# Attention weights transposed on TensorE instead of by DMA, and the division by the row sum moved behind the product with v

## The chip, the cores and the metric

The kernel runs on one core of one Trainium2 chip. The metric is device time in microseconds (us), the median of several executions. Engines are named as in the profile: PE (TensorE, matrix products and transposes, written to PSUM), PEld (its weight loads), DVE (VectorE), ACT (ScalarE), POOL (GpSimd, which here works only on SBUF) and SP (SyncE, which issues the DMAs).

## The reference

Attention with a causal window of 128 and a linear bias by head, then two gated feed-forward blocks over the 2304 tokens.

```python
# q, k, v: (4, 8, 576, 64); window = 128
scores = scale * np.matmul(q, k.transpose(0, 1, 3, 2))
mask = (rel >= 0) & (rel < window)
scores = np.where(mask, scores + bias[None], -1000000000.0)
scores = scores - np.max(scores, axis=-1, keepdims=True)
attn = np.exp(scores)
attn = attn / (np.sum(attn, axis=-1, keepdims=True) + 1e-09)
x = np.matmul(attn, v)            # then to (2304, 512)
x = (x @ w_a * (x @ w_b)) @ w_out                 # d_ff 1536
out = (x @ w1 * (x @ w2)) @ w3 @ moe2_w_out       # d_ff 1024
```

## The kernel before

**Attention.** A unit is one batch and one pair of heads, so there are 16. A unit has 576 queries: four blocks of 128 and a last one of 64. Blocks are taken in runs, (0, 1), (2, 3) and (4,), three to a unit, 48 in all. For a block of queries only one or two blocks of 128 keys lie in the window. The two heads are `j`; for the last block both heads share the 128 partitions.

- `prep` (L268 to L273) transposes the raw q and k of the next unit on PE and splits them into a high and a low part.
- `scores` (L311) makes three products per block and head. `step_exps` (L337, L343) adds the bias, finds the row maximum on DVE, and takes exponentials on ACT with their row sums in `st`. The tile `pe` holds the exponentials in float32, queries on partitions.
- `norms` (L356, L359) makes the reciprocal of the row sums, times 2^15 (`PSC`).
- `probs` (L371 to L382) multiplies the exponentials by it and splits them into two float16 parts in the tile `pp`: the high part on ACT (L375; block 0 on DVE, L371), the low part on DVE (L377). One DMA transpose per block (L382, on SP's queue) turns `pp` into `pt`, with keys on partitions.
- `pv` (L408) multiplies with v, which is in three bfloat16 parts, in five products per head and key block. `pv_out` (L422, L423) scales by 2^-15 and splits the result into `x_hi` (ACT) and `x_lo` (DVE).

**What sets the order.** `attention_ops` makes steps, one per run. Step n holds the late operations of the step before, then scores and exponentials of run n, `probs` of run n-1, the transposes of `prep`, a slot for filler work (None), and `pv` of run n-`LAG`. In the slot, up to 2.4 us (`FILL`) of products of the first feed-forward group (L545, L571) are put in, for tokens whose attention is done. Conversions of the weights are spread over the steps. During the first three units `keep_warm` (L352) adds products that nothing uses. A scheduler then orders each engine's instructions by its own estimates of time. The PSUM pool `ps_t` has three buffers, used in turn by the tiles of `prep` and of `pv`.

**After attention** what is left of the first group follows, then the other nine groups in tiles of 512 tokens (L545, L582, L597), and the product of w3 with the last weight (L453, L461), all on PE with the splits on ACT, DVE and POOL.

Of the kernel before, what the change touches and what calls it, by code (L numbers as in the profile page):

```python
# [8 lines left out]
F32 = mybir.dt.float32  # L9
# [25 lines left out]
LAG = 3  # L35
# [7 lines left out]
def attention_moe_moe(ctx, tc, q, k, v, w_a, w_b, w_o, w_1, w_2, w_3, w_o2, out):  # L43
    nc = tc.nc
# [23 lines left out]
    def f32(ap):  # L68
        return ap.bitcast(F32)
# [284 lines left out]
    def norms(run):  # L354
        st = live.pop(run)
        nc.vector.tensor_scalar(  # L356
            out=st[:, 2], in0=st[:, 1], scalar1=1.0e-9, scalar2=1.0 / PSC, op0=ALU.add, op1=ALU.mult
        )
        nc.vector.reciprocal(out=st[:, 3], in_=st[:, 2])  # L359

    def probs(u, i):
        m, n, nb, nj = window(i)
        d = live[u, i]
        pe, st = d["pe"], d["st"][:, 3]
        pp = sm_p.tile([P, 2 * 2 * 2 * P], F16, name="pp", bufs=5)[:, 0:2 * nj * n].rearrange(
            "p (a b c) -> p a b c", a=nj, b=2
        )
# [24 lines left out]
    def pv(run):  # L392
# [258 lines left out]
    def attention_ops():  # L651

        late = []
        for n in range(NR + LAG):
# [5 lines left out]
            if 1 <= n <= NR:  # L660
                ops.append(lambda r=runs[n - 1]: norms(r))
# [17 lines left out]
            if n >= LAG:  # L679
                ops.append(lambda r=runs[n - LAG]: pv(r))  # L680
# [51 lines left out]
    warm = sm_p.tile([P, 8 * P], F16, name="pt", bufs=6)[:, 0:2 * P]  # L732
# [64 lines left out]
```

## Time and profile before

| what | value |
|---|---|
| median of three runs | 1004.87 us (1002.13 to 1005.45) |
| the profiled execution, first to last instruction | 1003.0 us |
| PE busy over the span | 961.5 us (96%) |
| DVE, ACT, POOL busy | 532.3, 430.6, 400.7 us |
| PE busy, 0 to 80 us | 65.5 us, granted clock 0.68 |
| PE busy, 80 to 250 us (rest of attention) | 149.3 us, granted clock 0.94 |
| PE busy, 330 to 1003 us | 668.8 us of 673, granted clock 1.00 |

The profiled execution has no time of its own beside its span; the span of 1003.0 us lies within the three runs, 1.9 us under their median. Attention takes the first 250 us. A clock of 1.00 is 2.4 GHz, 0.50 is 1.2 GHz. The record of a product has a modelled end which runs into the next, so that a short stall between products doesn't show as idle time. Idle time of an engine counts where the chain of work that ended last runs through it.

### The profile page before, as it was taken

How to read it: one execution, taken by the hardware profiler on the slowest of the kernel's cores; microseconds unless marked ns; L12 is line 12 of the kernel's file. 1: busy time of each engine (PE TensorE's matmuls, PEld its weight loads, DVE VectorE, ACT ScalarE, POOL GpSimd, SP SyncE). 2: the span in 40 equal slices, each digit the busy share in tenths (PEclk: the TensorE clock that was granted, in tenths of full speed). 3: DMA queues.
4: the chain of work that ended last, by engine and by line, in shares of the span. 5: the costliest groups of instructions: out<-in, count | busy, mean ns of one | idle time of the engine just before them, and what ended most of it. 6: DMA issues, size and time to landing. Idle time of an engine off the chain costs nothing.

```text
span 1003.0 us, 16251 instructions
## 1 busy us (share of the span) xinstructions
PE 961.5 (96%) x6162; PEld 803.7 (80%) x6162; DVE 532.3 (53%) x1188; ACT 430.6 (43%) x1003; POOL 400.7 (40%) x329
## 2 busy tenths in 40 slices
PE   7889898888999999999999999999999999999998
PEld 6558787777988788888888888888888888888886
DVE  5979777764689634556474462442442442422222
ACT  5768767765654434434443341343421321311110
POOL 4344212211687423545462362574741631511111
PEclk6769998988999999999999999999999999999999
DMA  5897786864433222323331240120120220000012
GB/s 128 165 185 154 145 137 138 148 119 69 147 106 115 85 85 95 95 74 105 103 118 63 73 128 22 42 84 1 42 85 1 61 66 1 22 1 1 29 64 97
DMA packets 160078, 85.21 MB, mean 85 GB/s; under 512 B 128000, under 2 KB 148992, under 8 KB 160000
## 3 DMA queue, kind: packets, MB, share of 16 engines
q1 hardware_dynamic: 160000, 84.18, 34.0%
q8 instruction: 48, 0.79, 0.3%
q14 instruction: 30, 0.25, 0.1%
HBM read 58.20 MB, written 8.91 MB: 67 GB/s over the span
## 4 chain that ended last, share of the span: by engine, by line
PE 81%; DMA 6%; DVE 6%; issue 3%; ACT 3%; POOL 1%; SPq 1%; DVEq 0%; POOLq 0%; ACTq 0%
PE mm L545 44%; PE mm L582 11%; PE mm L597 10%; PE mm L461 4%; DMA pt<-pp 4%; PE s L311 3%; PE tr L408 3%; PE tr L268 2%; PE mm L571 1%; DVE pp L377 1%; DVE ca L121 1%; DMA raw<-in_moe_w_a 1%; DVE ca L114 1%; DVE ca L117 1%; POOL ca L126 1%
## 5 line engine op out<-in xcount | busy, mean ns | idle before, releaser
L72 POOL TENSOR_TENSOR gl<-g,gh 128x512 fp32r<-128x512 f32 (+1 forms) x108 | 124.5, 1153 | 316.2 <-ACT gh L555 301.8
L552 DVE TENSOR_TENSOR g<-a,mm 128x512 f32<-128x512 f32 (+1 forms) x108 | 64.1, 594 | 214.9 <-PE mm L545 193.6
L126 POOL TENSOR_TENSOR ca<-ca,ce 128x512 int32<-128x512 int32 x76 | 101.2, 1332 | 141.6 <-ACT ce L110 65.9
L555 ACT ACTIVATE gh<-g 128x512 fp32r<-128x512 f32 (+1 forms) x108 | 60.2, 558 | 176.4 <-DVE g L552 176.2
L545 PE MATMUL mm<-x_hi,wlA 128*128 128x512 f32 (+1 forms) x464 | 107.9, 351 | 0.0
L550 ACT ACTIVATE a<-mm 128x512 f32<-128x512 f32 (+1 forms) x108 | 55.9, 519 | 121.0 <-PE mm L545 120.9
L545 PE MATMUL mm<-x_lo,whA 128*128 128x512 f32 (+1 forms) x464 | 104.2, 345 | 0.0
L545 PE MATMUL mm<-x_hi,whA 128*128 128x512 f32 (+1 forms) x464 | 103.0, 343 | 0.0
L545 PE MATMUL mm<-x_hi,wlB 128*128 128x512 f32 (+1 forms) x400 | 99.3, 370 | 2.1 <-DVE g L552 0.8
L545 PE MATMUL mm<-x_lo,whB 128*128 128x512 f32 (+1 forms) x400 | 98.6, 368 | 0.0
L545 PE MATMUL mm<-x_hi,whB 128*128 128x512 f32 (+1 forms) x400 | 98.1, 368 | 0.0
L114 DVE TENSOR_SCALAR ca<-ca 128x512 f32<-128x512 f32 x76 | 47.3, 622 | 91.6 <-ACT ca L107 89.4
L545 PEld LDWEIGHTS mm<-x_hi,wlA 128*128 128x128 f32 x464 | 77.9, 192 | 11.1 <-issue 0.4
L545 PEld LDWEIGHTS mm<-x_lo,whA 128*128 128x128 f32 x464 | 78.1, 192 | 10.6
L545 PEld LDWEIGHTS mm<-x_hi,whA 128*128 128x128 f32 x464 | 77.3, 191 | 10.3
L545 PEld LDWEIGHTS mm<-x_hi,wlB 128*128 128x128 f32 x400 | 70.8, 188 | 16.0 <-DVE g L552 1.2
L586 DVE TENSOR_TENSOR acc<-acc,mm 128x512 f32<-128x512 f32 (+1 forms) x100 | 62.0, 630 | 39.4 <-PE mm L582 39.1
L107 ACT ACTIVATE ca<-raw 128x512 f32<-128x512 f32 x76 | 50.6, 666 | 72.5 <-DMA raw<-in_moe_w 39.5
L121 DVE SCALAR_TENSOR_TENSOR ca<-raw,ca 128x512 int32<-128x512 int32 x76 | 80.6, 1060 | 1.8
L545 PEld LDWEIGHTS mm<-x_lo,whB 128*128 128x128 f32 x400 | 71.1, 188 | 12.8
L545 PEld LDWEIGHTS mm<-x_hi,whB 128*128 128x128 f32 x400 | 71.0, 189 | 12.6
L110 ACT ACTIVATE ce<-raw 128x512 int32<-128x512 uint32 x76 | 50.8, 669 | 60.0 <-POOL ca L126 25.0
(104 smaller groups left out, 1873.4 us busy)
## 6 DMA issues: line engine op xcount, KB each, us to landing
raw<-in_moe_w SPq DMA_DIRECT2D x32, 512.0 KB, 3.7
raw<-in_moe_w_out SPq DMA_DIRECT2D x20, 512.0 KB, 3.5
raw<-in_moe_w_a SPq DMA_DIRECT2D x12, 512.0 KB, 3.6
raw<-in_moe_w_b SPq DMA_DIRECT2D x12, 512.0 KB, 3.7
out<-acc SPq DMA_DIRECT2D x18, 256.0 KB, 2.0
q_raw<-in_q SPq DMA_DIRECT2D x32, 128.0 KB, 2.8
k_raw<-in_k SPq DMA_DIRECT2D x32, 128.0 KB, 2.7
v_raw<-in_v SPq DMA_DIRECT2D x32, 128.0 KB, 2.7
```

What stands on the lines that cost most here:

```text
L72: eng.tensor_tensor(out=out, in0=a, in1=b, op=ALU.subtract)
L110: nc.scalar.activation(e, lw, ACTF.Copy, scale=2.0 ** -29)
L114: nc.vector.tensor_scalar(out=a, in0=a, scalar1=bits(0x38000000), scalar2=None, op0=ALU.max)
L121: nc.vector.scalar_tensor_tensor(out=ai, in0=hw, scalar=-(1 << 30), in1=ai, op0=ALU.bitwise_and, op1=ALU.bitwise_or)
L126: nc.gpsimd.tensor_tensor(out=ai, in0=ai, in1=es[0], op=ALU.add)
L545: nc.tensor.matmul(p, w[:, z, kk, :], x[:, kk, o], start=(y == 0), stop=(y == len(terms) - 1))
L550: nc.scalar.activation(a, ps[0], ACTF.Copy)
L552: nc.vector.tensor_tensor(out=gg, in0=a, in1=ps[1], op=ALU.mult)
L555: nc.scalar.activation(gh, gg, ACTF.Copy)
L582: nc.tensor.matmul(p, w, x, start=(y == 0), stop=(y == len(terms) - 1))
L586: nc.vector.tensor_tensor(out=ya, in0=ya, in1=p, op=ALU.add)
L597: nc.tensor.matmul(p, x, w, start=(y == 0), stop=(y == len(terms) - 1))
```

## The change

`probs` no longer multiplies by the reciprocal and no longer goes through a DMA. PE transposes the float32 exponentials into a PSUM tile of `ps_t`, in pieces of 128 by 128. ACT reads that tile, scales by 2^15 and writes the high float16 part. DVE reads it again and writes the low part. `norms` moves to just ahead of `pv` of the same run; POOL then copies the reciprocals out along 64 columns for each head (`rb`). `pv` starts each block with a PE transpose of `rb` into the right half of its own PSUM tile. `pv_out` copies that half to SBUF (`rt`, DVE), multiplies the product by it (`y`, DVE), and splits `y` into `x_hi` (ACT) and `x_lo` (now POOL, helper `sub`). `LAG` is 2 instead of 3.

```diff
-LAG = 3
+LAG = 2
...
     def norms(run):
         st = live.pop(run)
         nc.vector.tensor_scalar(
-            out=st[:, 2], in0=st[:, 1], scalar1=1.0e-9, scalar2=1.0 / PSC, op0=ALU.add, op1=ALU.mult
+            out=st[:, 2], in0=st[:, 1], scalar1=1.0e-9, scalar2=PSC, op0=ALU.add, op1=ALU.mult
         )
         nc.vector.reciprocal(out=st[:, 3], in_=st[:, 2])
+        k = st.shape[2]
+        rb = sm_p.tile([P, 2 * P], F32, name="rb")[:, 0:max(k, 2) * D]
+        nc.gpsimd.tensor_copy(
+            out=rb.rearrange("p (k d) -> p k d", k=k),
+            in_=st[:, 3].unsqueeze(2).to_broadcast([P, k, max(2 // k, 1) * D]),
+        )
...
     def probs(u, i):
...
-                nc.scalar.activation(pp[:, j, 0, :], pe[:, j, :n], ACTF.Copy, scale=st[:, j:j + 1])
-        for j in range(nj):
-            nc.vector.scalar_tensor_tensor(
-                out=pp[:, j, 1, :], in0=pe[:, j, :n], scalar=st[:, j:j + 1], in1=pp[:, j, 0, :],
-                op0=ALU.mult, op1=ALU.subtract,
-            )
-        t = sm_p.tile([P, 8 * P], F16, name="pt", bufs=6)[:, 0:2 * nj * n]
-        nc.sync.dma_start_transpose(
-            out=t.rearrange("p (g m) -> p g m", m=P), in_=pp.rearrange("p a b c -> p (a b c)")
-        )
...
+        ps = ps_t.tile([P, W], F32, name="tr")[:, 0:nj * n]
+            for g in range(nb):
+                o = (j * nb + g) * P
+                nc.tensor.transpose(ps[:, o:o + P], pe[:, j, g * P:(g + 1) * P], ident)
+        t = d["pt"] = sm_p.tile([P, 2, W], F16, name="pt", bufs=6)
+        hi, lo = t[:, 0, 0:nj * n], t[:, 1, 0:nj * n]
+        nc.scalar.activation(hi, ps, ACTF.Copy, scale=PSC)
+        nc.vector.scalar_tensor_tensor(out=lo, in0=ps, scalar=PSC, in1=hi, op0=ALU.mult, op1=ALU.subtract)
...
+            nc.tensor.transpose(ps[:, 2 * P + at:3 * P + at], d["rb"], ident)
...
-        nc.scalar.activation(x_hi[:, hp, o], ps, ACTF.Copy, scale=1.0 / PSC)
-        nc.vector.scalar_tensor_tensor(
-            out=x_lo[:, hp, o], in0=ps, scalar=1.0 / PSC, in1=f32(x_hi[:, hp, o]),
-            op0=ALU.mult, op1=ALU.subtract,
-        )
+        if m > LAST:
+            nc.vector.tensor_copy(out=r, in_=ps[:, 2 * P:2 * P + m])
...
+        nc.vector.tensor_tensor(out=y, in0=ps[:, :m], in1=r, op=ALU.mult)
+        nc.scalar.activation(x_hi[:, hp, o], y, ACTF.Copy)
+        sub(nc.gpsimd, x_lo[:, hp, o], y, f32(x_hi[:, hp, o]))
...
-                ops.append(lambda r=runs[n - 1]: norms(r))
...
+                ops.append(lambda r=runs[n - LAG]: norms(r))
                 ops.append(lambda r=runs[n - LAG]: pv(r))
```

Lines of the changed kernel: L377 are the transposes of `pe`, L380 and L381 the split, L396 the transpose of `rb`, L405 the products with v, L421 or L425 the copy, L427 the product, L428 `x_hi`. L548 and L574 are the filler products that were L545 and L571.

How the order moves. On PE, in the middle of attention, a stretch from one product with v to the next scores. Before, between the last product with v and the next filler (`tr<-ident,k_raw` is `prep`'s transpose, `s` a tile of scores):

```order
L408 MATMUL tr<-pt,v_raw_96 64x128
L268 MATMUL tr<-ident,k_raw_112 128x128 x3
L311 MATMUL s<-qkl,qkh 128x128 x2
L311 MATMUL s<-qkh 128x128 x2
L311 MATMUL s<-qkh,qkl 128x256 x2
L311 MATMUL s<-qkl,qkh 128x256 x2
L311 MATMUL s<-qkh 128x256 x2
L545 MATMUL mm<-x_hi,wlA_324 128x256
```

The same part of a step now:

```order
L405 MATMUL tr<-pt,v_raw_97 64x64
L377 MATMUL tr<-ident,pe 128x128 x4
L574 MATMUL mm<-gh,wlA_368 128x256
L311 MATMUL s<-qkh,qkl 128x128 x2
L377 MATMUL tr<-ident,pe 128x128 x4
L574 MATMUL mm<-gh,wlA_776 128x256
L574 MATMUL mm<-gl,whA_367 128x256
L268 MATMUL tr<-ident,k_raw_112 128x128 x3
L311 MATMUL s<-qkl,qkh 128x128 x2
L311 MATMUL s<-qkh 128x128 x2
```

Two groups of four transposes of `pe` stand among the scores and the fillers. Over the whole of attention the 256 transposes stand in 65 groups: 24 of four, 23 of two, 16 of six or eight.

On PE, inside one `pv`, between the products of its two blocks. Before:

```order
L408 LDWEIGHTS v_raw_96
L408 MATMUL tr<-pt,v_raw_96 64x128
L408 LDWEIGHTS v_1976
L408 MATMUL tr<-pt,v_1976 64x128
L408 LDWEIGHTS v_1976
```

Now, with the transpose of `rb`:

```order
L405 LDWEIGHTS v_raw_95
L405 MATMUL tr<-pt,v_raw_95 64x128
L396 MATMUL tr<-ident,rb 128x128
L405 LDWEIGHTS v_1826
L405 MATMUL tr<-pt,v_1826 64x128
```

A float32 transpose of the whole array now stands between two rows of products that use half of its columns. There are 80 of these; each is alone.

On DVE, one step in the middle of attention. Before (`pp` is the low part, `x_lo` the result of an earlier run):

```order
L377 SCALAR_TENSOR_TENSOR pp<-pe,st,pp 128x256
L377 SCALAR_TENSOR_TENSOR pp<-pe,st,pp 128x128 x2
L377 SCALAR_TENSOR_TENSOR pp<-pe,st,pp 128x256
L273 TENSOR_TENSOR qkl<-tr,qkh 128x512
L356 TENSOR_SCALAR st<-st 128x4
L359 RECIPROCAL st<-st 128x4
L356 TENSOR_SCALAR st<-st 128x1
L359 RECIPROCAL st<-st 128x1
L423 SCALAR_TENSOR_TENSOR x_lo<-tr,x_hi 128x256 x2
```

The same kind of step now:

```order
L421 COPY rt<-tr 128x256
L427 TENSOR_TENSOR y<-tr,rt 128x256
L381 SCALAR_TENSOR_TENSOR pt<-tr,pt 128x256
L381 SCALAR_TENSOR_TENSOR pt<-tr,pt 128x512
L555 TENSOR_TENSOR g<-a,mm 128x256
L425 COPY rt<-tr 64x64
L273 TENSOR_TENSOR qkl<-tr,qkh 128x512
L425 COPY rt<-tr 64x64
L427 TENSOR_TENSOR y<-tr,rt 128x64
L381 SCALAR_TENSOR_TENSOR pt<-tr,pt 128x512
```

DVE now reads PSUM tiles of `ps_t` in three kinds of instruction (the low part L381, the copy and the product of `pv_out`, and `prep`'s L273), where `prep` and `x_lo` did before.

## Rows read from the trace of the kernel before

**Rows 1.** The page: engine totals, and the granted clock in 40 slices of 25.1 us.

```profile
PE 961.5 (96%) x6162; PEld 803.7 (80%) x6162; DVE 532.3 (53%) x1188; ACT 430.6 (43%) x1003; POOL 400.7 (40%) x329
...
PEclk6769998988999999999999999999999999999999
```

**Rows 2.** Busy time by stretch: stretch, length, engines, granted clock, DMA share, GB/s.

```profile
0.00:80.00 80.00, 65.52 (x582) 47.46 (x584) 61.42 (x225) 55.58 (x168) 31.95 (x35) 0.68 0.83 159
80.00:250.00 170.00, 149.25 (x1944) 130.83 (x1939) 124.46 (x470) 121.44 (x385) 42.58 (x39) 0.94 0.72 130
250.00:330.00 80.00, 77.93 (x472) 68.16 (x470) 61.92 (x74) 43.51 (x82) 59.29 (x45) 1.00 0.40 126
330.00:1003.00 673.00, 668.83 (x3172) 557.21 (x3172) 284.50 (x421) 210.09 (x369) 266.92 (x211) 1.00 0.19 60
...
70.00:80.00 10.00, 10.00 (x97) 8.39 (x98) 6.52 (x32) 8.61 (x29) 1.37 (x2) 0.50 1.00 171
```

**Rows 3.** Chain that ended last, shares by line: 0 to 80 us, then 80 to 250.

```profile
by line: PE s L311 18.3%; PE tr L408 10.7%; PE tr L268 9.2%; DVE pp L377 8.3%; DMA pt<-pp 7.4%; DMA raw<-in_moe_w_a 5.7%; issue 4.9%; PE mm L352 4.3%; DMA k_raw<-in_k 3.4%; DVE qkl L273 2.8%; DVE ca L114 2.7%; DVE pe L337 2.7%; DVE ca L121 
...
by line: PE mm L545 21.7%; DMA pt<-pp 18.2%; PE tr L408 12.5%; PE s L311 10.4%; PE mm L571 8.7%; PE tr L268 6.3%; DVE pp L377 4.2%; issue 3.9%; DMA k_raw<-in_k 2.2%; DMA q_raw<-in_q 2.0%; ACT pe L343 1.7%; DVE pe L337 1.7%; ACT pp L375 1.4%
```

**Rows 4.** Pieces of that chain: start, us, engine, tile, line, count; first under half clock.

```profile
10.81 1.26 PE tr L268 x5
...
126.43 4.02 DMA pt<-pp
...
132.79 0.68 PE tr L408 x20
133.47 0.48 PE tr L268 x3
...
145.58 0.59 PE tr L268 x4
146.17 1.44 PE mm L571 x12
147.60 1.24 PE tr L408 x40
...
149.39 0.33 PE tr L268 x3
```

**Rows 5.** Waits in the whole span: who for whom, total us, times, longest.

```profile
PE tr L408 <- DMA pt<-pp: 18.4, 19, 1.8
PEld L408 <- issue: 17.7, 26, 2.6
...
PEld L408 <- DMA pt<-pp: 7.7, 8, 1.6
```

**Rows 6.** Instructions by line and shape: count, busy us, mean ns, idle before.

```profile
L377 DVE SCALAR_TENSOR_TENSOR pp<-pe,st,pp 128x256 f16<-128x256 f32 x112 | 58.6, 561 | 7.6 <-ACT pp L375 7.5
L375 ACT ACTIVATE pp<-pe,st 128x256 f16<-128x256 f32 x112 | 49.4, 499 | 8.9 <-DMA pt<-pp 4.7 <-DVE ca L121 1.1 <-ACT pe L343 0.9
L72 POOL TENSOR_TENSOR gl<-g,gh 128x256 fp32r<-128x256 f32 x36 | 28.9, 803 | 90.5 <-ACT gh L555 76.1 <-DMA k_raw<-in_k 14.4
L423 DVE SCALAR_TENSOR_TENSOR x_lo<-tr,x_hi 128x256 fp32r<-128x256 f32 x32 | 13.2, 414 | 4.0 <-ACT x_hi L422 3.8
L273 DVE TENSOR_TENSOR qkl<-tr,qkh 128x512 fp32r<-128x512 f32 x16 | 10.9, 680 | 1.6 <-ACT qkh L272 1.5
L272 ACT ACTIVATE qkh<-tr 128x512 fp32r<-128x512 f32 x16 | 9.4, 590 | 7.1 <-PE tr L268 7.0
```

**Rows 7.** DMA issues by line: count, median us to landing.

```profile
pt<-pp SPq DMA_TRANSPOSE x80, 3.3
```

More of the change, by code (lines that the diff above doesn't have):

```diff
@@ L356, in norms @@
         nc.vector.tensor_scalar(
-            out=st[:, 2], in0=st[:, 1], scalar1=1.0e-9, scalar2=1.0 / PSC, op0=ALU.add, op1=ALU.mult
+            out=st[:, 2], in0=st[:, 1], scalar1=1.0e-9, scalar2=PSC, op0=ALU.add, op1=ALU.mult
         )
         nc.vector.reciprocal(out=st[:, 3], in_=st[:, 2])
+        k = st.shape[2]
[4 more added lines that the diff above has]
+        )
+        for x, s in enumerate(run):
+            live[s]["rb"] = rb[:, x * P:(x + 1) * P]
     def probs(u, i):
@@ L363, in probs @@
         d = live[u, i]
-        pe, st = d["pe"], d["st"][:, 3]
-        pp = sm_p.tile([P, 2 * 2 * 2 * P], F16, name="pp", bufs=5)[:, 0:2 * nj * n].rearrange(
-            "p (a b c) -> p a b c", a=nj, b=2
-        )
+        pe = d.pop("pe")
+        ps = ps_t.tile([P, W], F32, name="tr")[:, 0:nj * n]
         for j in range(nj):
-            if i == 0:
-                nc.vector.tensor_scalar(
-                    out=pp[:, j, 0, :], in0=pe[:, j, :n], scalar1=st[:, j:j + 1], scalar2=None, op0=ALU.mult
-                )
-            else:
-                nc.scalar.activation(pp[:, j, 0, :], pe[:, j, :n], ACTF.Copy, scale=st[:, j:j + 1])
-        for j in range(nj):
-            nc.vector.scalar_tensor_tensor(
-                out=pp[:, j, 1, :], in0=pe[:, j, :n], scalar=st[:, j:j + 1], in1=pp[:, j, 0, :],
-                op0=ALU.mult, op1=ALU.subtract,
-            )
-        t = sm_p.tile([P, 8 * P], F16, name="pt", bufs=6)[:, 0:2 * nj * n]
-        nc.sync.dma_start_transpose(
-            out=t.rearrange("p (g m) -> p g m", m=P), in_=pp.rearrange("p a b c -> p (a b c)")
-        )
-        order = "p (a b c m) -> p a b c m" if nj == 2 else "p (b c a m) -> p a b c m"
-        d["pt"] = t, t.rearrange(order, a=2, b=2, c=nb)
+            for g in range(nb):
[5 more added lines that the diff above has]
+        nc.vector.scalar_tensor_tensor(out=lo, in0=ps, scalar=PSC, in1=hi, op0=ALU.mult, op1=ALU.subtract)
     ready = [0]
@@ L413, in pv @@
             if u < WARM_UNITS and m == P:
-                keep_warm(WARM, t[:, 0:4 * P])
+                keep_warm(WARM, t[:, 0, 0:nj * nb * P])
     def pv_out(run):
@@ L420, in pv_out @@
         o = slice(b * S + i * P, b * S + i * P + m)
-        ps = outs.pop(run)[:, :m]
-        nc.scalar.activation(x_hi[:, hp, o], ps, ACTF.Copy, scale=1.0 / PSC)
-        nc.vector.scalar_tensor_tensor(
-            out=x_lo[:, hp, o], in0=ps, scalar=1.0 / PSC, in1=f32(x_hi[:, hp, o]),
-            op0=ALU.mult, op1=ALU.subtract,
-        )
+        ps = outs.pop(run)
+        r = sm_p.tile([P, 2 * P], F32, name="rt")[:, :m]
+        if m > LAST:
+            nc.vector.tensor_copy(out=r, in_=ps[:, 2 * P:2 * P + m])
+        else:
+            for j in range(2):
+                c = slice(j * D, (j + 1) * D)
+                nc.vector.tensor_copy(out=r[c], in_=ps[c, 2 * P + j * LAST:2 * P + (j + 1) * LAST])
+        y = sm_p.tile([P, 2 * P], F32, name="y")[:, :m]
+        nc.vector.tensor_tensor(out=y, in0=ps[:, :m], in1=r, op=ALU.mult)
+        nc.scalar.activation(x_hi[:, hp, o], y, ACTF.Copy)
+        sub(nc.gpsimd, x_lo[:, hp, o], y, f32(x_hi[:, hp, o]))
         if hp == NP - 1:
@@ L731, in attention_moe_moe @@
     fl = Filler()
-    warm = sm_p.tile([P, 8 * P], F16, name="pt", bufs=6)[:, 0:2 * P]
+    warm = sm_p.tile([P, 2, W], F16, name="pt", bufs=6)[:, 0, 0:2 * P]
     nc.vector.memset(warm, 0.0)
```

6 lines of the change are left out of this document (4 added, 2 removed).

## The prediction

> **What bounds the kernel now.** I read the engine totals and the clock in slices first [rows 1]: PE is busy 96% of the span, and its granted clock is above 0.9 from the slice at 251 us on, but 0.6 to 0.8 in six of the ten slices before. The busy time by stretch [rows 2] parts the span in two. From 330 us PE is busy 668.8 of 673 us at clock 1.00; nothing there is touched by the change, and nothing that happens on other engines shortens it. The change lives in attention, the first 250 us. There PE is busy 65.5 of 80 us and 149.3 of 170 us, so it has 14.5 + 20.8 = 35 us of recorded idle time in all; its clock is 0.68 and 0.94. DVE has 61.4 + 124.5 = 186 us of work, ACT 177, POOL 75. What attention is late by at its end is paid at the end of the kernel, because PE has work without gaps afterwards. The converse holds too.
>
> Who ends last in attention is told by the chain [rows 3]. From 80 us on, the five listed PE lines make 59.6% of it, and the DMA transposes (pt<-pp) 18.2% of 170 = 30.9 us. Before 80 us the chain is a mixture: PE 42.5% in its three attention lines and L352, DVE's low part 8.3%, the DMA transposes 7.4% of 80 = 5.9 us. So PE is first in both stretches, and the DMA transposes are the largest single thing beside it: 37 us together. Their latency is 3.3 us [rows 7], and single ones stand in the chain with 4.02 us [rows 4].
>
> **The change part by part.** All of it is priced in the profiled execution, span 1003.0 us; the median of the runs is 1.9 us longer.
>
> *Added on PE: transposes of the exponentials.* A unit has 2 for block 0, 4 for each of blocks 1 to 3, and 2 for block 4: 16, in 16 units 256. They are of the same kind as `prep`'s (128x128 float32 against `ident`). Mean durations of such instructions contain the pipeline, so I price them by pieces of the chain that join without a gap [rows 4]: three cost 0.48 us between a product with v and scores (0.16 each), four 0.59 (0.15 each), three before filler products 0.33 (0.11 each). 256 of them are 28 to 41 us. By the order they stand in 65 groups of about four, some before scores, some before fillers; I take 0.13, or 33 us.
>
> *Added on PE: the transposes of `rb`*, five to a unit, 80 in all, each alone. One more transpose in a group costs 0.59 - 0.48 = 0.11 us, the first of a group 0.48 - 2 x 0.11 = 0.26. Twenty products with v take 0.62 to 0.68, so a lone transpose is worth eight of them. 33 of the 80 break a row of products with v and pay 0.26 (8.6 us); 47 stand where PE changes from another kind of work anyway, and I give them 0.11 (5.2 us). That is 14 us, with bounds 9 and 21.
>
> Here a rule speaks against the change. The Trainium skill, "TensorE: Matmul & The Clock Gate", Part 4: PE-mode transpose, gives about 275 ns for a 128x128 transpose in a kernel's context. At that price the 336 would be an estimated 92 us in place of 47. The groups in the chain show 0.11 to 0.26, so the trace does not agree for transposes in groups, and only nearly for single ones.
>
> *The clock.* In the first 80 us five to six of the 16 units run at a granted clock of 0.68 [rows 2], and five transposes cost 1.26 us under half clock [rows 4], 0.25 each. 5/16 of 47 is 14.7 us, which at 0.68 is 21.6: 7 us more. The bounds are 0 (full clock) and 15 (half clock all the time).
>
> *Removed: the DMA transposes.* The chain says 37 us. PE's own waits [rows 5] say less: 18.4 on PE and 7.7 on PEld are 26, and of another 17.7 ("issue", before the products with v) nobody is named. I take 30. The 80 transposes also leave SP's queue, and loads of q and k stop waiting behind them: 2.2% + 2.0% of 170 is 7 us of the chain from 80 us on [rows 3]; I take 5, bounds 0 and 7.
>
> *DVE and ACT.* For a block of 256 keys, two low parts at 0.561 become one of 512 read from PSUM, nearest to L273's 0.680; two high parts at 0.499 become one, nearest to L272's 0.590 [rows 6]. Over 48 such blocks DVE loses 21 us and ACT 20. Per pair of blocks `pv_out` puts two DVE instructions of about 0.41 in the place of one at 0.414, so 32 x 0.41 = 13 us comes back to DVE, and some 5 us for the last blocks. DVE nets about -10 to -18 of 186, ACT about -15 of 177. In the chain the two lines are worth 6.6 + 7.1 + 2.4 = 16 us [rows 3], but new ones stand in the same places: I take -3, bounds 0 and -10.
>
> *POOL* gains 32 subtractions at 0.803 [rows 6], 16 small ones and 48 copies, at most 0.8 each: about 26 + 6 + 38 = 70 us on 75, in 250. It stays the least loaded. But `pv` now waits for `rb`, behind which conversions and v's parts (POOL is in order) may be queued; that goes into the next term.
>
> *New waits.* The pool `ps_t` keeps three buffers, but where `prep` and `pv` took two tiles a step, `probs` now takes one or two more. A transpose can wait for the split of a tile three places earlier, and `pv` for POOL's copy. No row shows this; its bounds are 0, since fillers stand between in most steps, and 25, the DMA's own waits over again. I take 5, since DVE and ACT have become lighter and the splits take 1.3 us against the 3 to 4 us of a DMA.
>
> *`LAG` 2.* One step fewer at the end, 250/51 = 4.9 us, of which PE's work stays: -4, bounds 0 and -5. By the order 34 filler products (302 instead of 336) fall behind the end of attention, 34 x 0.12 = 4 us; PE does them either way, so this is zero for the sum.
>
> Sum: 33 + 14 + 7 - 30 - 5 - 3 + 5 - 4 = +17 us, span 1020, and with the 1.9 us about **1022 us**. A check from the other side: 54 us of added PE time do not fit into 35 us of recorded idle time, of which the start and the waits for exponentials remain. So PE has to end later unless its clock rises.
>
> **The rivals.**
>
> *PE stays at full clock (faster).* In the first 80 us a clock of 0.68 costs PE 0.32 x 80 = 26 us, and from 80 to 250 us 0.06 x 170 = 10 us [rows 2]. Between 70 and 80 us PE was busy all 10 us at clock 0.50, and the slices from 75 to 150 us show a clock of 0.9 or more [rows 1]. If the denser stream of the changed kernel is granted 1.0 in most of what was half clock, the 7 us above go and some 15 to 20 of the 36 come back: 1022 - 7 - 18 = 997. It decides from a mean clock of about 0.9 in the first 80 us. Against it: [rows 1] shows 0.6 to 0.7 in the first three slices although `keep_warm` puts in products there, and 0.8 again in three of the four slices from 150 to 250 us.
>
> *The PSUM buffers take the DMA's place (slower still).* If the tiles of `ps_t` wait for ACT and DVE as long as `pt` waited for its DMA, the term of 5 is 25: 1022 + 20 = 1042, and more if PE's clock falls with the gaps.
>
> *Neutral.* If all 35 us of idle time and the DMA's waits are one and the same and fill up exactly, PE's additions are covered: 1003 to 1008.
>
> *Transposes at 0.275 us each.* Priced as mechanism of this kernel by the highest lone price under half clock, 0.25 to 0.26, for all 336: 87 us instead of 47, 1022 + 40 = 1062. The page named above would have it so; the groups at 0.11 to 0.16 speak against it.
>
> **How the numbers follow.** Forecast 0.55 (1006 to 1036); full clock 0.22 (985 to 1002); PSUM buffers 0.16 (1036 to 1060); neutral 0.05; dear transposes 0.02. About 0.3%, 3 us, is what a measurement of this kernel can tell from no change: below 1002 is faster, above 1008 slower. Faster takes the clock's 0.22; same the neutral case and a little of the forecast's edge, 0.08; slower the rest, 0.70. The range leaves out half of the clock case below 994 and the upper part of the PSUM and dear cases above 1046.
>
> **What would show it.** In the profile after: PE busy from 0 to 250 us with less idle time than 35 us, and attention's last product with v some 15 us later; L377 and L396 together near 47 us of the PE's stream; no DMA in the chain of attention but loads; granted clock of the first 80 us near 0.7. The forecast is wrong on the fast side if that clock is above 0.9, or if groups of four transposes cost no more than 0.4 us; on the slow side if L377 or L396 wait for ACT, DVE or POOL for more than some 10 us in all. From 330 us before, or its counterpart after, nothing should differ.

## The result

The changed kernel takes **1017.88 us** (median of four runs, 1016.24 to 1019.03); the kernel before took 1005.16 us beside it (four runs, 1002.13 to 1005.82). The ratio is 1.0134, with a 95% interval of 1.0112 to 1.0156: 12.7 us slower. The execution that was profiled took 1017.48 us, with a span of 1015.7 us.

The page of the changed kernel, engine totals and granted clock in 40 slices of 25.4 us, to be read beside [rows 1]:

```profile
PE 990.5 (98%) x6498; PEld 823.8 (81%) x6498; DVE 531.6 (52%) x1156; ACT 422.7 (42%) x971; POOL 443.9 (44%) x425
...
PEclk9889999999999999999999999999999999999999
```

The first slices, which read 6, 7, 6, now read 9, 8, 8, and from the fourth on there is nothing under 9. The same by stretch, with the columns of [rows 2] (length, busy PE, PEld, DVE, ACT, POOL, granted clock, DMA share, GB/s):

```profile
0.00:80.00 80.00, 65.31 (x659) 48.22 (x660) 58.40 (x203) 52.29 (x154) 47.87 (x62) 0.91 0.50 122
80.00:250.00 170.00, 167.69 (x2079) 142.11 (x2077) 117.81 (x440) 111.23 (x352) 67.32 (x101) 1.00 0.23 51
250.00:330.00 80.00, 75.65 (x526) 65.16 (x525) 63.09 (x86) 45.35 (x93) 55.27 (x46) 1.00 0.37 112
330.00:1003.00 673.00, 672.90 (x3204) 561.48 (x3203) 287.46 (x422) 213.79 (x375) 272.88 (x217) 1.00 0.18 58
```

From 80 to 250 us PE is busy 167.69 of 170 us at clock 1.00, where [rows 2] has 149.25 at 0.94. In the first 80 us it is busy as long as before (65.31 against 65.52), but at 0.91 in place of 0.68. The DMA share has fallen from 0.83 to 0.50 and from 0.72 to 0.23. The chain that ended last, 0 to 80 us and then 80 to 250 us, against [rows 3]:

```profile
by line: PE s L311 14.4%; PE tr L377 9.7%; ACT pe L343 7.7%; PE tr L268 7.4%; DMA raw<-in_moe_w_a 6.6%; PE mm L352 6.5%; PE tr L405 6.1%; issue 4.4%; DVE ca L121 3.8%; DVE ca L114 3.5%; DMA k_raw<-in_k 3.2%; DVE pt L381 3.0%; ACT ca L107 3.
...
by line: PE mm L548 20.5%; PE tr L405 17.3%; PE s L311 16.3%; PE tr L377 11.5%; PE mm L574 9.9%; PE tr L268 7.3%; PE tr L396 6.0%; ACT pe L343 2.9%; DVE pe L337 1.3%; issue 1.2%; DVE qkl L273 1.0%; DVE st L356 0.9%; ACT pt L380 0.7%; DVE y 
```

In the second stretch the listed PE lines alone are 88.8%, and no DMA stands there any more. L377 is the transposition of the exponentials, L396 that of `rb`. In the first stretch ACT's exponentials (7.7%), loads and DVE's conversions stand between the pieces of PE, as they did before.

The last product of the exponentials with v, from the timeline of each kernel (start, us, engine, line), of before and then of after:

```profile
251.14 0.20 PE L408 MATMUL tr<-pt,v_raw 128*64 128x64 f16 x2
...
257.93 0.20 PE L405 MATMUL tr<-pt,v_raw 128*64 128x64 f16 x1
```

Attention ends 6.8 us later. Behind it, the first block of products of w3 with the last weight (L461 before, L464 after, twelve in a row in the chain) starts at 345.52 us before and at 358.06 us after:

```profile
345.52 2.78 PE mm L461 x12
...
358.06 2.77 PE mm L464 x12
```

That is 12.5 us. Behind this place both kernels are alike: 1003.0 - 345.5 = 657.5 us and 1015.7 - 358.1 = 657.6 us. So all of the loss arises before it: 6.8 us up to the end of attention, and 5.7 us from there to this place. In that second stretch the first products of the feed-forward groups, from which the fillers are taken (L545 before, L548 after), are these (stretch, length, PE busy and count, clock, DMA share, GB/s):

```profile
251.30:345.50 94.20, 63.52 (x336) 1.00 0.38 118
...
258.10:358.00 99.90, 67.52 (x370) 1.00 0.37 111
```

The 34 more are the filler products that the order no longer puts ahead of the last product with v. They are 4.0 us of the 5.7, so the work of attention is 10.8 us later rather than 6.8.

### The profile page after: what moved, and what is told of

It is laid out like the page before. It is cut to its first block, busy times and chain, and to the rows that moved or that the text cites. A ratio compares the mean times of both kernels' runs of the same rounds, so it can differ in the third digit from the quotient of the medians.

```text
span 1015.7 us, 16894 instructions
## 1 busy us (share of the span) xinstructions
PE 990.5 (98%) x6498; PEld 823.8 (81%) x6498; DVE 531.6 (52%) x1156; ACT 422.7 (42%) x971; POOL 443.9 (44%) x425
## 4 chain that ended last, share of the span: by engine, by line
PE 86%; DVE 5%; ACT 3%; DMA 3%; issue 1%; POOL 0%; SPq 0%; ACTq 0%; DVEq 0%
PE mm L548 44%; PE mm L585 11%; PE mm L600 10%; PE mm L464 4%; PE s L311 4%; PE tr L405 4%; PE tr L377 3%; PE mm L574 2%; PE tr L268 2%; PE tr L396 1%; ACT pe L343 1%; DVE ca L121 1%; DMA raw<-in_moe_w_out 1%; DVE ca L114 1%; DMA raw<-in_moe_w_a 1%
## 5 line engine op out<-in xcount | busy, mean ns | idle before, releaser
L548 PE MATMUL mm<-x_hi,wlA 128*128 128x512 f32 (+1 forms) x464 | 108.4, 348 | 0.0
L548 PE MATMUL mm<-x_lo,whA 128*128 128x512 f32 (+1 forms) x464 | 104.2, 343 | 0.0
L548 PE MATMUL mm<-x_hi,whA 128*128 128x512 f32 (+1 forms) x464 | 102.8, 342 | 0.0
L548 PE MATMUL mm<-x_hi,wlB 128*128 128x512 f32 (+1 forms) x400 | 99.3, 370 | 0.6 <-POOL wlB L72 0.5
L548 PE MATMUL mm<-x_lo,whB 128*128 128x512 f32 (+1 forms) x400 | 98.8, 368 | 0.0
L548 PE MATMUL mm<-x_hi,whB 128*128 128x512 f32 (+1 forms) x400 | 98.1, 368 | 0.0
L114 DVE TENSOR_SCALAR ca<-ca 128x512 f32<-128x512 f32 x76 | 50.3, 661 | 86.9 <-ACT ca L107 85.2
L548 PEld LDWEIGHTS mm<-x_lo,whA 128*128 128x128 f32 x464 | 77.3, 189 | 10.7
L548 PEld LDWEIGHTS mm<-x_hi,wlA 128*128 128x128 f32 x464 | 77.4, 189 | 10.4
L548 PEld LDWEIGHTS mm<-x_hi,whA 128*128 128x128 f32 x464 | 76.9, 189 | 10.4
L548 PEld LDWEIGHTS mm<-x_hi,wlB 128*128 128x128 f32 x400 | 70.9, 188 | 14.1 <-POOL wlB L72 0.9
L548 PEld LDWEIGHTS mm<-x_lo,whB 128*128 128x128 f32 x400 | 71.1, 188 | 12.8
L548 PEld LDWEIGHTS mm<-x_hi,whB 128*128 128x128 f32 x400 | 71.0, 189 | 12.6
L110 ACT ACTIVATE ce<-raw 128x512 int32<-128x512 uint32 x76 | 50.9, 670 | 60.1 <-DMA w<-ce 24.8
```

Source lines behind the costliest of these rows:

```text
L114: nc.vector.tensor_scalar(out=a, in0=a, scalar1=bits(0x38000000), scalar2=None, op0=ALU.max)
L548: nc.tensor.matmul(p, w[:, z, kk, :], x[:, kk, o], start=(y == 0), stop=(y == len(terms) - 1))
```

## The experiments

All times are medians of at least four runs, and a ratio is to the kernel before on the same chip (1004.83 us beside the first four kernels, 1002.86 beside the next four, 1004.56 beside the last four). Theory 1 is the prediction's: PE's stream sets the end of attention, so that what is added to it or taken from it is paid one for one. The rivals are that waits behind other engines, the lost clock or the DMA's latency set it.

| kernel | what differs | us | ratio (95%) | clock, 0 to 80 us | PE busy, 80 to 250 us | last product with v, us |
|---|---|---|---|---|---|---|
| before | | 1005.16 | 1 | 0.68 | 149.3 | 251.1 |
| after | | 1017.88 | 1.0134 (1.0112 to 1.0156) | 0.91 | 167.7 | 257.9 |
| a_rb_first | after, `rb` transposed in pairs | 1011.47 | 1.0064 (1.0040 to 1.0089) | 0.85 | 166.1 | 252.1 |
| a_no_rb | after, no division | 998.73 | 0.9943 (0.9923 to 0.9964) | 0.87 | 166.4 | 243.5 |
| a_tr_twice | after, each transposition twice | 1038.47 | 1.0336 (1.0312 to 1.0361) | 0.98 | 168.9 | 281.6 |
| b_dummy_tr | before, 256 unread transposes | 1019.43 | 1.0148 (1.0111 to 1.0184) | 0.98 | 159.3 | 263.7 |
| a_norm | after, division ahead of the transposition | 1019.23 | 1.0152 (1.0123 to 1.0181) | 0.81 | 160.6 | 265.5 |
| mix23 | a_norm, blocks 2 and 3 by DMA | 1019.41 | 1.0140 (1.0109 to 1.0171) | 0.84 | 159.4 | 264.2 |
| b_warm | before, more products that keep the clock up | 1008.16 | 1.0054 (1.0034 to 1.0073) | 0.79 | 151.5 | 253.1 |
| a_lag3 | after, `LAG` 3 | 1017.79 | 1.0134 (1.0113 to 1.0155) | 0.91 | 167.7 | 258.7 |
| b_no_dma | before, no transposition at all | 976.55 | 0.9713 (0.9696 to 0.9731) | 0.89 | 161.8 | 220.9 |
| b_lag2 | before, `LAG` 2 | 1018.59 | 1.0133 (1.0104 to 1.0162) | 0.81 | 148.6 | 261.1 |
| mixrb_lag3 | a_rb_first, blocks 2 and 3 by DMA, `LAG` 3 | 1000.62 | 0.9956 (0.9936 to 0.9975) | 0.77 | 164.4 | 247.8 |
| mixrb_lag2 | the same, `LAG` 2 | 1023.52 | 1.0184 (1.0139 to 1.0229) | 0.82 | 161.2 | 267.8 |

### What the added transposes cost

**a_tr_twice** does each transposition of the exponentials a second time into the same place:

```diff
-                nc.tensor.transpose(ps[:, o:o + P], pe[:, j, g * P:(g + 1) * P], ident)
+                for y in range(2):
+                    nc.tensor.transpose(ps[:, o:o + P], pe[:, j, g * P:(g + 1) * P], ident)
```

> The changed kernel with each of the 256 transposes of the exponentials made twice into the same place: 256 more, all behind another of their kind, at 0.11 us each at full clock. Theory 1 (PE's stream): 28 us more, less what falls into the first 80 us, where PE has some 15 us of idle time: 1036 to 1046 us. Theory 2 (waits): the added work fills gaps, 5 to 12 us more, 1023 to 1030.

It takes 1038.47 us, as theory 1 expected: 20.6 more than after, which is 80 ns for each of 256. That is three quarters of the 28 us which 256 pieces of 0.11 us make, so most of PE's added load is paid, and a quarter falls into gaps. Pieces of its chain (start, us, engine, tile, line, count):

```profile
110.62 0.59 PE tr L378 x4
122.08 1.02 PE tr L378 x8
```

and one of after's:

```profile
102.36 0.58 PE tr L377 x4
```

Four cost 0.58 or 0.59, eight 1.02: the further four are 0.43, or 0.11 each, as the prediction read them from `prep` in [rows 4].

**b_dummy_tr** adds the same 256 transposes to the kernel before, into a PSUM tile that nobody reads; its DMA transposes stay:

```diff
+        dm = mm_tile(W)[:, 0:nj * n]
+        for j in range(nj):
+            for g in range(nb):
+                o = (j * nb + g) * P
+                nc.tensor.transpose(dm[:, o:o + P], pe[:, j, g * P:(g + 1) * P], ident)
```

> The kernel before with the 256 transposes of the exponentials added into a PSUM tile that nothing reads; the DMA transposes and all else stay. Theory 1 (PE's added work is the price, and a denser PE gets the clock back that was lost before): 33 us of PE work more, up to 29 us of lost clock back (36 us lost before, 7 after the change), and the DMA's waits partly filled by the new work: 1010 to 1020 us. Rival (the DMA's 26 to 37 us of waits stand on the path beside PE's work, and only taking them away pays for the transposes): 33 us more and little back, 1030 to 1040.

It takes 1019.43 us: 14.6 more than the kernel before, where the prediction's term is 33. Its stretches (length, PE, clock, DMA share, GB/s) and its longest wait of PE for a DMA:

```profile
0.00:80.00 80.00, 65.53 (x683) 0.98 0.82 160
80.00:250.00 170.00, 159.30 (x1948) 0.96 0.68 124
...
PE tr L413 <- DMA pt<-pp: 8.9, 10, 2.4
```

The granted clock of the first 80 us rises from 0.68 to 0.98 with nothing changed but these transposes, and PE waits 8.9 us for the DMA transposes where [rows 5] has 18.4. In those 80 us PE is busy no longer than before (65.53 against 65.52) though 80 of the transposes stand there; from 80 to 250 us it is busy 10 us longer. So more than half of the forecast 33 us was paid by clock and gaps; how much by which was not separated.

### What the division after the product costs

**a_no_rb** leaves out the division by the sum: no `rb`, none of its 80 transposes, no copy of it out of PSUM. `pv_out` only scales by `1.0 / PSC`:

```diff
-            nc.tensor.transpose(ps[:, 2 * P + at:3 * P + at], d["rb"], ident)
...
-        nc.vector.tensor_tensor(out=y, in0=ps[:, :m], in1=r, op=ALU.mult)
+        nc.vector.tensor_scalar(out=y, in0=ps[:, :m], scalar1=1.0 / PSC, scalar2=None, op0=ALU.mult)
```

> The changed kernel without the division: rb, its copy on POOL, its 80 transposes on PE and the copy rt on DVE are left out, and y is the product times a constant. Theory 1 (PE's stream): 33 lone transposes at 0.38 and 47 at about 0.2 go, 12.5 + 9.4 = 22 us, so about 996 to 1000 us. Theory 2 (waits): the copy on DVE and the wait for POOL go too, but of PE's 22 us less than half is seen, about 1007 to 1012.

998.73 us, 19.2 less than after and 6.1 less than before. A kernel has to divide somewhere, so this one only measures: with the transposition on TensorE and no division there is a gain, and the way the division is done turns it into a loss. What the 80 transposes, POOL's copy and DVE's `rt` each have of the 19.2 us was not separated.

**a_rb_first** keeps the division, but transposes the `rb` of both blocks of a run ahead of the run's products:

```diff
+        for x, s in enumerate(run):
+            nc.tensor.transpose(ps[:, (2 + x) * P:(3 + x) * P], live[s]["rb"], ident)
...
-            nc.tensor.transpose(ps[:, 2 * P + at:3 * P + at], d["rb"], ident)
```

> The changed kernel with both transposes of rb of a run ahead of the products with v of both blocks, so that 32 of the 80 no longer break a row of products. In the changed kernel such a lone one holds PE 0.15 + 0.26 = 0.41 us from the product before it to the one behind it, where two products follow each other after 0.03; second in a group a transpose costs 0.11. Theory 1 (PE's stream sets the end of attention, from 80 us on without gaps): 32 x (0.38 - 0.11) = 8.6 us less, about 1009 to 1011 us. Theory 2 (waits between engines, for PSUM tiles and the splits, set the end, and PE only looks full): the work goes, the wait stays, at most 2 to 3 us less, about 1015.

1011.47 us, 6.4 less than after: a third of the price of the division, for the order of two instructions. Why is seen in the chain, first of after, then of a_rb_first:

```profile
107.00 0.26 PE tr L396
107.25 0.40 PE tr L405 x10
107.66 0.26 PE tr L396
107.92 0.68 PE tr L405 x20
...
105.86 0.37 PE tr L392 x2
106.22 0.96 PE tr L406 x30
...
111.10 0.22 PE tr L392 x2
111.31 1.24 PE tr L406 x40
```

In after each of the two stands alone and costs 0.26. The row of products behind it starts anew: 10 products take 0.40 and 20 take 0.68, so a further product costs 0.028 and the start of a row 0.12. Two rows with two transposes and 30 products take 1.60 us. In a_rb_first two transposes and 30 products take 0.37 + 0.96 = 1.33 us at one place, and 0.22 + 1.24 = 1.46 us with ten products more at another. 32 runs have such a pair; 0.27 us for each is the 8.6 us of theory 1, and 6.4 / 32 = 0.2 us is what each saves in the end.

**a_norm** divides ahead of the transposition. The exponentials of one head are multiplied on POOL, those of the other on DVE, and there is no `rb`; `norms` stands one step after the exponentials again, and `pv_out` splits as before the change, with `x_lo` on DVE:

```diff
+        for j in range(nj):
+            eng = (nc.gpsimd, nc.vector)[j]
+            eng.tensor_scalar(out=pe[:, j, :n], in0=pe[:, j, :n], scalar1=st[:, j:j + 1], scalar2=None, op0=ALU.mult)
...
-            nc.tensor.transpose(ps[:, 2 * P + at:3 * P + at], d["rb"], ident)
```

> Transposes on PE as in the changed kernel, but the exponentials are multiplied by the reciprocal of their sum before they are transposed (head 0 on POOL, head 1 on DVE, in place); rb, its transposes, rt and y are gone, and the split of the product with v is that of the kernel before. Theory 1 (PE's stream sets the end): PE has the same work as where the division was left out, 998.7 us, so 997 to 1003. Theory 2 (waits): each transpose now waits for POOL or DVE behind the exponential, in queues that also hold conversions and v's parts, 1005 to 1013.

1019.23 us, no better than after, though PE has the transposes of a_no_rb only: 20.5 us are lost elsewhere. The waits of PE (who for whom, total us, times, longest), and POOL's multiplication by form:

```profile
PE s L311 <- ACT qkh L272: 7.5, 5, 4.6
PE tr L268 <- DVE x_lo L414: 5.8, 5, 3.1
PE tr L372 <- POOL pe L367: 3.4, 1, 3.4
...
L367 POOL TENSOR_SCALAR pe<-pe,st 128x256 f32<-128x256 f32 x64 | 60.5, 952 | 35.1 <-ACT pe L343 12.2 <-DVE st L359 6.2 <-ACT pt L375 5.0
```

PE's idle time from 0 to 250 us is 18.3 + 9.4 = 27.7 us, against 17.0 in after. The multiplications stand on DVE and POOL, where other work that PE waits for stands too, and the granted clock is lower as well (0.81 and 0.96 in the two stretches, against 0.87 and 1.00 in a_no_rb). Which of this bears how much of the 20.5 us was not separated. Both theories missed it, with 1013 at most. That the multiplications delay what is queued behind them on DVE and POOL is the likely reading; no run shows it by itself.

### What the DMA transposes cost

**b_no_dma** takes the DMA transposes out of the kernel before: the products read `pp` itself, so the exponentials stay untransposed.

```diff
-        t = sm_p.tile([P, 8 * P], F16, name="pt", bufs=6)[:, 0:2 * nj * n]
-        nc.sync.dma_start_transpose(
-            out=t.rearrange("p (g m) -> p g m", m=P), in_=pp.rearrange("p a b c -> p (a b c)")
-        )
+        t = pp.rearrange("p a b c -> p (a b c)")
```

> The kernel before without its 80 DMA transposes: the products with v read the tile pp as it stands, so the transposition is left out and all else stays, LAG 3 and the waits for the splits included. By the forecast's terms (30 us of waits and 5 us of loads go): about 968 us. Theory 1 (PE's stream, with a clock that follows its density): PE's waits of 26 us go, and the clock regains part of the 36 us; 960 to 975. Rival (the DMA's latency lies mostly beside DVE's, ACT's and PE's own work, and another wait ends next): 12 to 20 us less, 983 to 992.

976.55 us, 28.0 less than before: between the two expectations, and 7 less than the 35 of the prediction's two terms. The chain from 80 to 250 us shows what stands in it now:

```profile
by line: DVE pp L377 17.1%; PE mm L542 16.9%; DVE pe L337 8.8%; PE tr L405 7.4%; PE s L311 5.5%; DVE qkl L273 4.1%; issue 3.8%; PE mm L568 3.7%; PE tr L268 3.3%; ACT pe L343 3.2%; DVE x_lo L420 2.9%; DMA raw<-in_moe_w_out 2.4%; DMA raw<-in_
```

DVE's low parts, 4.2% of that chain in [rows 3], are now 17.1% and its largest member. By this chain, waits for DVE stood behind the waits for the DMA.

**b_lag2** and **a_lag3** exchange the distance, in steps, between a run's exponentials and its products with v:

```diff
-LAG = 3
+LAG = 2
```

> The kernel before with LAG 2 in place of 3. If the DMA's latency is what LAG 3 covers: PE's waits for pt grow from 26 us to about double, 1015 to 1035. If a step is long enough for splits and DMA (a step takes some 5 us, the DMA 3 to 4): within 4 us of before, 1000 to 1008.

> The changed kernel with LAG 3 in place of 2. Theory 1 (PE's stream): PE has the same work and one step more to run out at the end, 0 to 5 us more, 1018 to 1023. Theory 2 (waits): the products with v get one step more of room for the splits and for rb, and the waits of PE (some 10 us beyond 0.15 us each) shrink, 1008 to 1014.

With `LAG` 2 the kernel before takes 1018.59 us, 14.0 more, and PE waits somewhat longer for the transposes:

```profile
PE tr L408 <- DMA pt<-pp: 23.0, 17, 3.3
```

23.0 us in 17 waits against 18.4 in 19 [rows 5], the longest 3.3 us, as long as one takes to land by the median [rows 7]. These 4.6 us are a third of the 14.0, and not the doubling that was expected; the rest wasn't traced. The changed kernel takes 1017.79 us with `LAG` 3 (a ratio of 1.0134, the same as after's): the third step is worth nothing to it, neither way.

### The clock

**b_warm** puts more unread products into the kernel before, four a block in six units, where it has two in three:

```diff
-WARM_UNITS, WARM = 3, 2
+WARM_UNITS, WARM = 6, 4
```

> The kernel before with more of the products that nothing uses: four a block in the first six units in place of two in the first three, 96 in place of 24, 72 x 0.216 = 15.5 us more PE work at full clock. If the clock that PE lost in the first 80 us of the kernel before (0.68) stood on the path: the granted clock rises above 0.9 and the time falls to 990 to 1000. If the first 80 us are set by other things (loads of weights, DVE, the DMA transposes): the clock rises and the time stays or grows, 1004 to 1015.

1008.16 us, 5.3 more than before. The first 80 us:

```profile
0.00:80.00 80.00, 65.74 (x605) 43.99 (x605) 63.75 (x216) 53.66 (x162) 32.74 (x36) 0.79 0.77 159
```

The clock rises from 0.68 to 0.79, not to the 0.9 that the first expectation asked for, and PE is busy 65.7 us again. By 80 us 340 products with v and 134 of scores are done, against 338 and 147 before: the higher clock has brought the kernel no further. How much of the 72 products fell into gaps in any case was not separated.

These clocks are of one execution each. The mean clock of the whole span, which is known for every execution, lies between 0.962 and 0.983 in the kernel before (31 executions), between 0.975 and 0.986 in b_warm, between 0.981 and 0.991 in b_dummy_tr, and between 0.991 and 0.993 in after. So b_warm's clocks overlap with those that the kernel before shows by itself; after's don't.

### A kernel that takes both ways

**mix23** is a_norm with the blocks 2 and 3 of each unit sent through the DMA as before (`DMA_BLOCKS = (2, 3)`, `LAG` 2), the other blocks transposed by TensorE:

```diff
+        if i in DMA_BLOCKS:
+            pp = sm_p.tile([P, 2 * 2 * 2 * P], F16, name="pp", bufs=5)[:, 0:2 * nj * n].rearrange(
+                "p (b a c) -> p b a c", a=nj, b=2
+            )
...
+            nc.sync.dma_start_transpose(
+                out=t.rearrange("p h (g m) -> p (h g) m", m=P), in_=pp.rearrange("p b a c -> p (b a c)")
+            )
+            return
```

> As a_norm, but the run of blocks 2 and 3 of each unit goes the way of the kernel before (split first, then a DMA transpose), the runs (0, 1) and (4,) are transposed on PE: 128 of the 256 transposes, at 0.13 us, leave PE, 32 DMA transposes return. Theory 1 (PE's stream): 998 to 1003 less 16 us where the DMA's latency lies beneath the denser work of PE, so 984 to 992. Rival (the DMA's waits return to the path, and the clock falls with them): a third to a half of the 30 us of waits before comes back, 996 to 1006.

1019.41 us: the gain expected of it is not there. PE is busy only 54.1 of the first 80 us, its largest sums of waits are for DVE, 5.2 to 5.8 us each (for `x_lo`, `qkl` and `pt`), and it shares a_norm's multiplications, so it tells nothing of the mixture by itself. **mixrb_lag3** and **mixrb_lag2** therefore mix without them: blocks 0, 1 and 4 as in a_rb_first, blocks 2 and 3 normalised ahead of the DMA and split as before the change (with two buffers of `pp` in place of five), and `LAG` at 3 or 2.

```diff
+DMA_BLOCKS = (2, 3)
...
-                ops.append(lambda r=runs[n - LAG]: norms(r))
+                if not by_dma(runs[n - LAG]):
+                    ops.append(lambda r=runs[n - LAG]: norms(r))
```

> LAG 3, both transposes of rb first. The run of blocks 2 and 3 goes the way of the kernel before (scaled, split, DMA transpose, no rb); the runs (0, 1) and (4,) go the way of the changed kernel. Against a_rb_first (1011.5 us) 128 transposes at 0.13 and 32 of rb at about 0.2 leave PE, 23 us, and 32 DMA transposes return. Theory 1 (PE's stream): 988 to 996 if the DMA lies beneath PE's work. Theory 2 (waits, with DVE and ACT carrying both kinds of split in order): 1000 to 1010.

> The same with LAG 2: the DMA of a run has one step less. Theory 1: 988 to 998, within 4 us of LAG 3. Theory 2: PE waits for pt, 5 to 15 us more than with LAG 3.

With `LAG` 3 it takes 1000.62 us (997.67 to 1003.75, seven runs), a ratio of 0.9956 (0.9936 to 0.9975): 17 us faster than after and, by 0.4%, faster than the kernel before. That lies in the range of theory 2: against a_rb_first 23 us of PE's work were to go, and 11 us of time went. With `LAG` 2 it takes 1023.52 us, 23 more, which neither theory expected. In its longest wait for a transposition PE stands 5.2 us:

```profile
PE tr L432 <- DMA pt<-pp: 6.1, 3, 5.2
```

Those waits are 6.1 us of the 23; the rest wasn't traced to a wait of its own.

## Why the prediction was right, and where it was right by cancellation

The sign and the size were forecast (1022 us against 1017.88, with an interval of the ratio that lies above 1). Most terms stayed within their bounds, but several values were off, in both directions: the transposes of the exponentials, the DMA's waits and the clock were taken too high, the division and the end's step of `LAG` too low. By the runs below, an estimate, the errors are some 12 us (transposes) and 6 us (clock, which by the prediction's own working makes 1.5 us at 0.91) on the one side, and 7 (DMA), 5 (division) and 4 (`LAG`) on the other. That they nearly cancel is luck.

**PE as the bound** held from 80 us on: PE is idle 2.3 of 170 us there. In the first 80 us it is not shown to be the bound: PE is idle 14.7 us there, as against 14.5 before. PE's recorded idle time from 0 to 250 us fell from 35 us to 14.7 + 2.3 = 17.0, as the last part of the prediction asked, and what a_tr_twice adds to PE and a_no_rb takes from it moved the end by 20.6 and 19.2 us. What the prediction called the check from the other side (54 us of added time into 35 us of gaps) describes it best.

**Transposes of the exponentials, forecast 33 (28 to 41).** The price of a piece was right: 0.58 and 0.59 for four, with 0.15 read from [rows 4]. As a cost in time it is too high: 20.6 us by a_tr_twice, 14.6 by b_dummy_tr. A sum over the chain of 0 to 250 us has 9.7% of 80 and 11.5% of 170, 27.3 us. The Trainium skill, "TensorE: Matmul & The Clock Gate", Part 4: PE-mode transpose, gives about 275 ns for a 128x128 transpose of bfloat16 in one kernel's context; at that price the 256 would be an estimated 256 x 0.275 = 70 us. The trace doesn't agree for these float32 transposes in groups, where a_tr_twice has 80 ns for each more, and only the lone ones come near it with 0.26.

**Transposes of `rb`, forecast 14 (9 to 21).** 19.2 us for the whole division, near the upper bound. In the chain of after, 0 to 250 us, the transposes themselves are 4.8%, 12.0 us, and together with those of the exponentials 39 us, where 47 were forecast:

```profile
by line: PE s L311 15.7%; PE mm L548 14.0%; PE tr L405 13.7%; PE tr L377 10.9%; PE tr L268 7.3%; PE mm L574 6.7%; PE tr L396 4.8%; ACT pe L343 4.4%; issue 2.2%; DMA raw<-in_moe_w_a 2.1%; PE mm L352 2.1%; DVE pe L337 1.7%; DVE pt L381 1.4%; 
```

The term priced the 0.26 of a lone transposition, but not the 0.12 us with which the interrupted row starts again: 33 x 0.12 = 4 us. That makes 16 of the 19.2; the rest stays open. Here the by-form group of them (count, busy us, mean ns, idle before), first of after, then of a_rb_first:

```profile
L396 PE MATMUL tr<-ident,rb 128*128 128x128 f32 x80 | 24.8, 310 | 2.5 <-DVE st L359 1.6 <-DVE qkl L273 0.7 <-DVE pt L381 0.2
...
L392 PE MATMUL tr<-ident,rb 128*128 128x128 f32 x80 | 17.6, 285 | 3.6 <-DVE st L359 1.6 <-DVE y L428 0.9 <-DVE qkl L273 0.7
```

Busy time falls from 24.8 to 17.6 us by their order alone.

**The clock, forecast +7 with the transposes at 0.68.** Wrong. The granted clock of the first 80 us came out at 0.91, above the 0.9 from which the rival "full clock" was to decide, and the prediction said that it would then be wrong on the fast side. It was not, because the rival's price was wrong too: it took time lost at a lower clock for time lost on the path. Products with v done by 80 us, their busy time and the clock, of before and of after, and then the transposes that after has done in the same time, of the exponentials and of `rb` (stretch, length, PE busy and count, clock, DMA share, GB/s):

```profile
0.00:80.00 80.00, 15.99 (x338) 0.68 0.83 159
...
0.00:80.00 80.00, 12.82 (x340) 0.91 0.50 122
...
0.00:80.00 80.00, 13.54 (x70) 0.91 0.50 122
...
0.00:80.00 80.00, 6.16 (x19) 0.91 0.50 122
```

340 products with v stand against 338, with 89 transposes more and a third more clock. That is not level, since `LAG` 2 lets them come a step sooner: a_lag3 has 300 by then. And of scores the changed kernel has done fewer, 135 against 147 (before, then after):

```profile
0.00:80.00 80.00, 27.08 (x147) 0.68 0.83 159
...
0.00:80.00 80.00, 18.68 (x135) 0.91 0.50 122
```

A unit has 27 of them and 90 products with v, and the 16 units take 250 us, so 12 scores or 38 products with v are some 7 us, an estimate. So much the changed kernel is behind at 80 us, though its clock is a third higher: the clock paid for a part of these transposes at most and gave nothing beyond.

What PE has to do moves this stretch little. The last product of scores of the fifth unit and the first of the sixth, of before and after, and then the first of the sixth in a_no_rb and in a_tr_twice (start, us, engine, line):

```profile
73.94 0.41 PE L311 MATMUL s<-qkh 128*128 128x256 f32 x1
75.49 0.47 PE L311 MATMUL s<-qkh,qkl 64*128 64x128 f32 x2
...
77.20 0.28 PE L311 MATMUL s<-qkh 128*128 128x256 f32 x1
85.22 0.33 PE L311 MATMUL s<-qkh,qkl 64*128 64x128 f32 x2
...
83.35 0.33 PE L311 MATMUL s<-qkh,qkl 64*128 64x128 f32 x2
...
86.75 0.33 PE L311 MATMUL s<-qkh,qkl 64*128 64x128 f32 x2
```

After is 3.3 to 9.7 us later than before here. Each transposition done twice adds 1.5 us, of 20.6 at the end; the division left out takes away 1.9 us here (5.7 at the fifth unit's last scores, at 71.54), of 19.2 at the end. The chain of that stretch names loads, exponentials and conversions beside PE, and PE waits there for tiles of `ps_t` (new waits, below). Which of them makes the changed kernel late was not tried, and whether all of that is carried to the end isn't shown: b_warm has 134 products of scores by 80 us and ends 5.3 us later. In b_dummy_tr, where these parts are those of the kernel before, 149 products of scores are done by 80 us, against 147 before: there the clock paid for all.

**DMA waits and loads, forecast -35 (-26 to -44).** -28.0 by b_no_dma, within the bounds; what the term missed, by that run's chain, is that waits for DVE's low parts stand right behind those for the DMA. The removal and the added transposes also share the same gaps: taken one by one they are -28.0 and +14.6, together -13.4, but a_no_rb, which has both and more, gains 6.1.

**DVE and ACT, forecast -3**, was not measured by itself. The new splits cost what was assumed: 589 ns for ACT's and 687 for DVE's, on blocks of 128x512, against 590 and 680 taken from [rows 6]:

```profile
L381 DVE SCALAR_TENSOR_TENSOR pt<-tr,pt 128x512 f16<-128x512 f32 x48 | 32.6, 687 | 11.7 <-ACT pt L380 11.2
L380 ACT ACTIVATE pt<-tr 128x512 f16<-128x512 f32 x48 | 28.0, 589 | 10.0 <-PE tr L377 9.6
```

**New waits, forecast 5 (0 to 25).** Over the whole span not far off, but they stand in one place. The waits of L377 and L396, all of 1.6 us and more, and then PE's wait for the DMA in the first 80 us of the kernel before:

```profile
PE tr L377 <- DVE y L427: 3.8, 3, 1.8
PE tr L377 <- DVE pt L381: 2.7, 2, 1.5
PE tr L377 <- DVE qkl L273: 2.0, 1, 2.0
PE tr L396 <- DVE st L359: 1.6, 1, 1.6
...
PE tr L408 <- DMA pt<-pp: 4.9, 5, 1.8
```

With the smaller ones they are 12.0 us in the whole span, a little above the 10 that the prediction allowed, where [rows 5] has 18.4 of PE for the DMA transposes. But 9.8 of the 12.0 fall into the first 80 us (3.5 of the first line's 3.8, and all of the next three lines). Of these, 8.2 us end with DVE instructions that read tiles of `ps_t`, where waits of 4.9 us for the DMA went. So the rival that PSUM's buffers take the DMA's place came about there in part; from 80 us on it did not, with 13.5 us of waits for the DMA gone (18.4 - 4.9) and 2.2 new. No run gave `ps_t` another buffer, so what these waits cost stays open.

**`LAG`, forecast -4.** 0, by a_lag3. One step fewer at the end was counted as a gain, but PE has work in it either way. What the prediction did not see is that the distance is worth 14 us to the kernel before (b_lag2), of which PE's waits for the DMA show 4.6, and nothing to the changed one; the change gives up a dependence on it rather than gaining a step.

**The fillers, forecast zero.** The 34 products did move as the order said, and cost 4.0 us behind attention in place of in it, so zero for the sum was right. The prediction's "15 us later" for the last product with v didn't allow for them; it is 6.8, and 10.8 with them.

The measured terms make 20.6 + 19.2 - 28.0 = +11.8 of the 12.7 us, or 14.6 + 19.2 - 28.0 = +5.8, according to which kernel prices the transposes. They aren't additive, and which share of the gaps each uses stays open.

## What to carry to other kernels

Moving a transposition from the DMA to TensorE pays only for what the DMA's latency really holds up, and it is paid in TensorE's stream: measure both apart, one kernel with the removal and one with an unread copy of the addition. A transposition that stands alone in a row of narrow products cost 0.38 us with the row's new start, one more in a group 0.11: collect them ahead of the row. Don't count a low granted clock as time lost before the chain shows that engine there: in the first 80 us of this kernel added work brought up the clock and the kernel no further.

## What was not expected of the hardware

- Transposes of 128x128 float32 added to PE's work raised the granted clock: 0.68 to 0.98 in the first 80 us, 80 of them there (b_dummy_tr); 0.91 in after. With 40 more float16 products in the same stretch it was 0.79 (b_warm), and without any transposes added it was 0.81 in b_lag2 and 0.89 in b_no_dma.
- In a row of products with v, which use 64 of the 128 columns of the array, each further one costs 0.028 us; a transposition between them costs 0.26, and the row's next start 0.12. In a group a further transposition costs 0.11.
- POOL took 0.952 us to multiply 128x256 float32 by a scalar per partition in place (a_norm), but 0.418 to copy a tile of the same size out of a broadcast operand (line L362 of after):

```profile
L362 POOL COPY rb<-st 128x256 f32<-128x256 f32 x32 | 13.4, 418 | 45.9 <-PE tr L396 27.6 <-DVE st L359 15.8 <-issue 1.5
```
